# Sliding-window attention and a SiLU feed-forward: q and k of the first two batches loaded in two parts, with a new written order

## The chip, the cores and the metric

The kernel runs on one core of a Trainium2 chip. The metric is device time in microseconds (us) of one execution, the median over runs. Engines are called PE (TensorE, matmuls), PEld (its weight loads), ACT (ScalarE), DVE (VectorE), POOL (GpSimd) and SP (SyncE). POOL issues all loads and SP all stores.

## The reference

Causal attention in a window of 64 tokens, over 8 batches, 8 heads, 576 tokens and a head size of 64, is followed by a two-matrix feed-forward on the 4608 tokens:

```python
scores = scale * np.matmul(q, k.transpose(0, 1, 3, 2))
mask = (rel >= 0) & (rel < 64)              # rel = query position - key position
attn = softmax(np.where(mask, scores, -1e9))
x = np.matmul(attn, v)                      # -> [4608, 512], heads side by side
h = x @ w_in                                # w_in  [512, 2048]
return (h * sigmoid(h)) @ w_out             # w_out [2048, 512]
```

All inputs and the output are float32. The kernel loads its inputs with a cast to bfloat16.

## The kernel before

**Tiles.** A block is 64 tokens; a batch has 9 blocks, and all 8 batches make 72 blocks, numbered through. Blocks 0 to 8 are batch 0, and 9 to 17 batch 1. A token tile j is 512 tokens, or 8 blocks, so there are nine (tile 0 holds blocks 0 to 7, tile 1 blocks 8 to 15). Four heads form a quad; quad 0 and quad 1 are called a0 and a1 here.

**Attention.** A visit treats some blocks of one quad: `scores` (PE, L292; with an added mask from L285 in the first visits), four exponentials (`expo`, ACT, L307), `masking` (DVE, L314, where the mask was not added), `values` (PE, L323), `inverse` (DVE, L334), `normal` (DVE, L338) and `turn_out` (DVE, L442), which transposes the result into `xt`, the input of the feed-forward. Tiles 0 and 1 are visited in halves of four blocks, later tiles in eight. `values` needs v in a layout with two neighbouring blocks on the 128 partitions; for the first two batches `place_all` (L273, L275; on ACT or DVE) copies halves of the loaded v to make the other half of these pairs.

**Loads of q and k.** For batches 0 and 1, `load_quad` (L224) brings q or k of four heads in one load: partition p of a head's 32 gets 18 successive tokens. `turn_quad` then transposes it on DVE into `kT` (L255) or `qT` (L258). All blocks of that batch and quad depend on this one transpose. For later batches `load_head` (L227) brings one head at a time and `turn_blocks` (L265, L268) transposes four. `load_v`, `load_v_even` (L233 to L241) bring v, `load_w_in` (L245) and `load_w_out` (L248) the weights, each weight in eight loads of 256 KB as they lie in SBUF.

**Feed-forward.** Tile 0 takes the plain product: `first_plain` (PE, L450), 16 silus (ACT, L461), `second_plain` (PE, L464). The first four groups of `first_plain` are cut in two halves; the first half needs only quad 0 of the attention and the first half of w_in's rows. Tiles 1 to 8 take a scheme with seven products of half size in place of eight: `first_product` (PE, L507), `second_product` (PE, L519), with sums of the weights (`weight_sum1`, `weight_sum2`, DVE, L469, built once), of tokens (`token_sum1`, `token_sum2`, DVE, L485 to L496), copies and sums of partial results (`fork` L523, `join` L526) and silus (L529). The stores are at L533.

**The order.** Nothing is scheduled when the kernel runs. Each step is an operation with a number, an engine and dependencies, added to `Plan`; the string `ORDER` then names the operations in the order in which they are written to the engines' queues, with the PSUM banks (of eight) that each takes. `74P7` is operation 74, on PE, in bank 7. An engine works through its own operations in this order, and waits where a dependency isn't met. The string `LOADS` only numbers the loads and transposes of the start and adds them to the plan:

```python
LOADS = "p0-2 u0-4 i0-2 i2-4 i4-6 r0-1 i6-8 o0-2 v0-1 o2-3 r1-2 o3-4 v1-2 u4-5 o4-5 v2-4 o5-8 v4-5"
```

Here p is q and k of batch 0 (by quads), r those of batch 1, u and v the value blocks of batches 0 and 1, i w_in, and o w_out. Before the first scores PE is given filler matmuls (`warm`, L895), which compute nothing that is used. A check of the inverses at the end may call `general()`, a slow path for extreme inputs, which these inputs don't take.

Of the kernel before, what the change touches and what calls it, by code (L numbers as in the profile page):

```python
# [29 lines left out]
class Plan:  # L30
# [88 lines left out]
def kernel(ctx, tc, q, k, v, w_in, w_out, out):  # L119
# [414 lines left out]

    SOFT, ROWS, VACT, F1, F2 = 0.69, 1, 2, 1, 1
    turned, placed = {}, {}
    score_ops, value_ops, turn_ops = {}, {}, {}
    cast_ops = []  # L540
# [447 lines left out]
```

## Time and profile before

| what | value |
|---|---|
| median of 3 runs | 277.21 us (275.41 to 277.24) |
| profiled execution | 276.81 us, its span 275.0 us |
| PE busy | 264.7 us (96%) |
| DVE busy | 214.0 us (78%) |
| ACT busy | 195.6 us (71%) |
| POOL busy | 129.7 us (47%) |
| loads (POOL's queue) | 21.51 MB, in 96128 packets |

In rows of the timeline the first number is the start in us from the start of the span, the second the duration, then the engine, the line, the operation and what it writes and reads; "x24" counts merged instructions, and brackets hold the idle time of the engine before the row and what ended it. The granted PE clock is 1.000 throughout.

### The profile page before, as it was taken

To read this page: it belongs to the slowest core of one execution; us is meant where nothing else is said; L and a number is where in the kernel's file an instruction comes from. 1 tells how busy PE (TensorE), PEld (TensorE's weight loads), DVE (VectorE), ACT (ScalarE), POOL (GpSimd) and SP (SyncE) were. 2 spreads that over 40 slices of the span, in tenths; PEclk is the share of its full clock that TensorE was granted. 3 is DMA by queue.
4 is the path that set the end of the run, shared out by engine and by line. 5 is a ranking of instruction groups with operands and counts; after the bars stand their busy time and mean duration, and the time that the engine had idled before them with its cause. 6 is when DMAs were issued, how large, how long until landed. Compare 5 with 4: busy or idle time off the path is not lost.

```text
span 275.0 us, 10018 instructions
## 1 busy us (share of the span) xinstructions
PE 264.7 (96%) x4335; PEld 218.0 (79%) x4342; DVE 214.0 (78%) x426; ACT 195.6 (71%) x361; POOL 129.7 (47%) x194
## 2 busy tenths in 40 slices
PE   7978999999999999999999999999999999999993
PEld 2557844688888888888888888888888888888882
DVE  3757578999996898889799999988867967824741
ACT  1555993699749993987499958893888489537910
POOL 7944566988959758596387335940000000000000
PEclk9999999999999999999999999999999999999999
DMA  6999999999999959999979998990400040003004
GB/s 106 167 190 210 198 191 172 144 198 157 118 151 209 127 56 97 242 122 87 93 179 159 83 126 122 136 121 2 155 0 2 6 155 0 2 29 127 0 2 157
DMA packets 101631, 31.62 MB, mean 115 GB/s; under 512 B 92368, under 2 KB 95440, under 8 KB 101584
## 3 DMA queue, kind: packets, MB, share of 16 engines
q0 software_dynamic: 96128, 21.51, 86.1%
q1 hardware_dynamic: 5456, 9.44, 9.7%
q8 instruction: 35, 0.57, 0.9%
q14 instruction: 12, 0.10, 0.1%
HBM read 42.99 MB, written 9.44 MB: 191 GB/s over the span
## 4 chain that ended last, share of the span: by engine, by line
PE 88%; ACT 4%; DVE 4%; issue 1%; ACTq 0%
PE room L519 36%; PE room L507 35%; PE room L292 4%; PE room L323 4%; PE room L450 4%; PE room L895 4%; PE room L464 2%; ACT es L307 2%; DVE o L338 1%; ACT L307 1%; ACT g L461 1%; DVE es L314 1%; DVE xt L442 1%; PE room L285 1%; ACT L461 0%
## 5 line engine op out<-in xcount | busy, mean ns | idle before, releaser
L529 ACT ACTIVATE g<-room 128x512 bf16<-128x512 f32 x96 | 53.6, 605 | 4.5 <-PE room L507 4.1
L507 PEld LDWEIGHTS <-wsum 128*128 128x128 bf16 x512 | 49.9, 98 | 7.2 <-issue 1.0
L519 PEld LDWEIGHTS <-gsum 128*128 128x128 bf16 x512 | 49.1, 98 | 6.2 <-DVE gsum L496 0.2
L507 PE MATMUL room<-xsum,wsum 128*128 128x256 bf16 x384 | 53.3, 272 | 0.5 <-ACT es L307 0.3
L307 ACT ACTIVATE es<-room 128x512 bf16<-128x512 f32 (+1 forms) x88 | 39.1, 533 | 14.2 <-PE room L292 9.6
L519 PE MATMUL room<-wsum,gsum 128*128 128x256 bf16 x384 | 48.4, 273 | 0.0
L507 PEld LDWEIGHTS <-w_in_sb 128*128 128x128 bf16 x384 | 37.2, 98 | 4.7
L519 PEld LDWEIGHTS <-g 128*128 128x128 bf16 x384 | 36.7, 98 | 4.6
L526 DVE TENSOR_TENSOR room<-room,part 128x512 f32<-128x512 f32 (+1 forms) x41 | 27.8, 684 | 13.7 <-ACT part L523 3.5
L227 POOL DMA_DIRECT2D nat<-in_k_dram x48 | 30.0, 631 | 15.1 <-DVE kT L265 11.4
L507 PE MATMUL room<-xt,w_in_sb 128*128 128x256 bf16 x256 | 36.8, 273 | 0.0
L519 PE MATMUL room<-w_out_sb,g 128*128 128x256 bf16 x256 | 35.7, 273 | 0.0
L227 POOL DMA_DIRECT2D nat<-in_q_dram x48 | 29.9, 637 | 9.7 <-DVE qT L268 6.1
L523 ACT COPY ot<-room 128x512 f32<-128x512 f32 (+1 forms) x23 | 13.3, 582 | 28.6 <-PE room L519 21.5
L235 POOL DMA_DIRECT2D vv<-in_v_dram x32 | 29.6, 940 | 5.0 <-DMA nat<-in_k_dram 1.7
L523 ACT COPY room<-room 128x512 f32<-128x512 f32 x40 | 23.3, 592 | 12.1 <-PE room L507 10.8
L526 DVE TENSOR_TENSOR fin<-room,part 128x512 f32<-128x512 f32 x32 | 21.6, 683 | 9.0 <-PE room L507 6.1
L523 ACT COPY part<-room 128x512 f32<-128x512 f32 x40 | 23.6, 598 | 6.4 <-PE room L519 3.2
L241 POOL DMA_DIRECT2D vv<-in_v_dram x24 | 22.3, 934 | 12.0 <-PE room L323 11.5
L314 DVE TENSOR_TENSOR es<-es,strip 128x1024 bf16<-128x1024 bf16 (+1 forms) x36 | 21.9, 626 | 6.7 <-ACT es L307 6.4
L338 DVE TENSOR_TENSOR o<-room,recips 128x896 bf16<-128x896 f32 (+2 forms) x36 | 25.9, 726 | 0.8
L496 DVE TENSOR_TENSOR gsum<-g,gsum 128x512 bf16<-128x512 bf16 x64 | 25.1, 415 | 0.4
(75 smaller groups left out, 376.8 us busy)
## 6 DMA issues: line engine op xcount, KB each, us to landing
out_dram<-ot SPq DMA_DIRECT2D x16, 512.0 KB, 3.9
vv<-in_v_dram POOLq DMA_DIRECT2D x56, 128.0 KB, 5.0
nat<-in_k_dram POOLq DMA_DIRECT2D x48, 72.0 KB, 4.0
nat<-in_q_dram POOLq DMA_DIRECT2D x48, 72.0 KB, 3.7
w_in_sb<-in_moe_w_in_dram POOLq DMA_DIRECT2D x8, 256.0 KB, 9.2
w_out_sb<-in_moe_w_out_dram POOLq DMA_DIRECT2D x8, 256.0 KB, 9.0
nat<-in_k_dram POOLq DMA_DIRECT2D x4, 288.0 KB, 8.0
nat<-in_q_dram POOLq DMA_DIRECT2D x4, 288.0 KB, 8.2
```

The costliest lines, as they stand in the source:

```text
L227: queue[e].dma_start(out=nats[b % 2][a][kk][32 * h:32 * h + 32].rearrange("p (n x) -> p n x", n=NB), in_=(q, k)[kk][b, 4 * a + h].rearrang ...
L235: queue[e].dma_start(out=vv[b % 2][:, :, 2 * g + 1, 0:D], in_=v[b, :, 128 * g:128 * g + 128].rearrange("h p d -> p h d"))
L241: queue[e].dma_start(out=vv[b % 2][:, :, 2 * g, 0:D], in_=v[b, :, 128 * g - 64:128 * g + 64].rearrange("h p d -> p h d"))
L307: nc.scalar.activation(out=es_part(a, blocks)[:, h], in_=banks[bank.idx][:, 0:64 * n], func=ACTF.Exp, scale=scale)
L314: nc.vector.tensor_mul(t, t, strip[:, s:s + n].rearrange("k n i -> k (n i)").unsqueeze(1).to_broadcast([128, 2, 64 * n]))
L338: nc.vector.tensor_mul(out, at_values(bank, n)[:, :, :, 0:D], recips[:, w:w + 2 * n].rearrange("k (t n) -> k t n", t=bank.wide).unsqueeze( ...
L496: nc.vector.tensor_sub(out=dst[2 * i - 1], in0=g(1, 2 - i), in1=dst[i - 1])
L507: nc.tensor.matmul(banks[bank.idx][:, 256 * i:256 * i + 256], lhsT=lhs(z, i), rhs=rhs(z), start=(start and i == 0 and z == 0), stop=(z == ...
L519: nc.tensor.matmul(banks[bank.idx][:, 256 * m:256 * m + 256], lhsT=lhs(m, i), rhs=rhs(i), start=(start and i == 0 and m == 0), stop=(stop ...
L523: copies[e](out=dst, in_=src)
L526: nc.vector.tensor_add(out=dst, in0=bank, in1=part)
L529: nc.scalar.activation(out=g_tile(pair, 256 * t, 256 * t + 256), in_=src.rearrange("k (f t) -> k f t", f=2), func=ACTF.Silu)
```

## The change

**Two parts.** `load_quad` and `turn_quad` get a part. Of the 18 tokens per partition the first load would have held, the main part of batch 0 holds 16 (512 tokens, blocks 0 to 7), the rest 2 (64 tokens, block 8). For batch 1 the main part holds 14 (448 tokens, blocks 9 to 15) and the rest 4 (128 tokens, blocks 16 and 17). So eight loads and eight transposes are added (k and q, two quads, two batches), and each block depends on its own part alone. A rest of batch 0 writes 256 bytes per partition, one of batch 1 512.

**Weight sums in wider pieces.** `weight_sum1` and `weight_sum2` work on 1024 elements per partition in place of 512: 8 operations each in place of 16.

**A new order.** All of `ORDER` is different. The loads as POOL issues them at the start (q1 a0 is q of batch 1, quad 0; w_in 0-2/1 is columns 0 to 511 of the second half of the rows; v0 g2 is the third value load of batch 0; "rest" is a second part):

```
before: k0 a0, q0 a0, k0 a1, q0 a1, v0 g2, v0 g0, v0 g1, v0 g3, w_in 0-2/0, 0-2/1, 2-4/0, 2-4/1, 4-6/0, 4-6/1,
        k1 a0, q1 a0, w_in 6-8/0, 6-8/1, w_out 0, 2, k1 a1, w_out 4, v1 g0, q1 a1, v1 g1, w_out 6, v0 g4, w_out 8,
        v1 g2, w_out 10, v1 g3, w_out 14, 12, then batch 2
after:  k0 a0, q0 a0, k0 a1, q0 a1, v0 g2, v0 g0, v0 g1, v0 g3, w_in 0-2/0, 2-4/0, k0 a1 rest, w_in 0-2/1, 2-4/1,
        q1 a0 rest, w_in 4-6/1, q0 a1 rest, w_in 6-8/1, 4-6/0, q0 a0 rest, w_in 6-8/0, k1 a0, q1 a0, k0 a0 rest,
        w_out 0, 2, v0 g4, w_out 4, v1 g2, k1 a1, q1 a1, w_out 6, v1 g1, w_out 8, v1 g3, v1 g0, w_out 10,
        k1 a1 rest, w_out 14, 12, q1 a1 rest, k1 a0 rest, then batch 2
```

PE at the start (S scores, V values, a0 and a1 the quads, numbers the blocks; "first" is `first_plain`, "second" `second_plain`):

```
before: 24 fillers, S a0 0-3, S a0 4-7, 7 fillers, S a1 0-3, S a1 4-7, 4 fillers, V a0 0-3, V a1 0-3, V a0 4-7,
        first (2 halves, with 1 filler), V a1 4-7, first ..., S a0 8-11, first (4 groups), second of tile 0 with
        S a0 12-15, S a1 8-11, V a0 8-11, V a1 8-11, V a0 12-15, S a1 12-15, V a1 12-15 between them
after:  23 fillers, S a0 0-3, S a0 4-7, 4 fillers, S a1 0-3, S a1 4-7, 4 fillers, V a0 0-3, 2 fillers, V a1 0-3,
        V a0 4-7, V a1 4-7, 1 filler, first (4 halves), all other first, second of tile 0 with S a0 12-15,
        S a0 8-11, S a1 12-15, S a1 8-11, V a0 8-11, V a0 12-15, V a1 8-11, V a1 12-15 between them
```

On ACT the exponentials of batch 1 stood among the silus of tile 0 (12 silus, 3 exponentials, 4 silus, the other exponentials); now all 16 silus come first. On DVE the main transposes of batch 1 and the rests of batch 0 now stand among the sums of w_in and the masks of blocks 8 to 15; q of quad 0 is the first rest of batch 1 to be transposed there, and the other three (k of quad 1, k of quad 0, q of quad 1, in this order) stand among the normalizations of blocks 8 to 15. The later tiles keep their operations; their order and banks differ in many places.

The diff without `ORDER`, cut to its core:

```diff
-    wsum1 = [keep.tile([128, 4, 2, 256], BF16, name=f"wsum1{u}") for u in range(4)]
+    wsum1 = [keep.tile([128, 4, 2, 512], BF16, name=f"wsum1{w}") for w in range(2)]
...
-    def load_quad(e, b, a, kk):
-        queue[e].dma_start(out=nats[b % 2][a][kk], in_=(q, k)[kk][b, 4 * a:4 * a + 4].rearrange("h (p c) d -> (h p) (c d)", c=18))
+    def quad_part(b, rest):
+        most = (16, 14)[b]
+        return (most, 18 - most) if rest else (0, most)
+
+    def load_quad(e, b, a, kk, rest):
+        c0, c = quad_part(b, rest)
+        queue[e].dma_start(out=nats[b % 2][a][kk][:, 64 * c0:64 * c0 + 64 * c],
+                           in_=(q, k)[kk][b, 4 * a:4 * a + 4, 32 * c0:32 * c0 + 32 * c].rearrange("h (p c) d -> h p (c d)", c=c))
...
+    def turn_quad(b, a, kk, rest):
+        c0, c = quad_part(b, rest)
+        src = nats[b % 2][a][kk][:, 64 * c0:64 * c0 + 64 * c].bitcast(FP32)
         if kk:
+            n = 64 + 576 * (b % 2) + 32 * c0
+            dst = kT[a][:, n:n + 32 * c].rearrange("x t y -> x (t y)").bitcast(FP32)
+            nc.vector.transpose(out=dst.rearrange("x (p c) -> x c p", c=c), in_=src.rearrange("x (c w) -> x c w", c=c))
...
-    def weight_sum1(i, u):
-        sum_op(i, [wsum1[u][:, n] for n in range(4)], w_in_part(0, 0, u), w_in_part(0, 1, u), w_in_part(1, 0, u), w_in_part(1, 1, u))
+    def weight_sum1(i, w):
+        part = lambda h, c: w_in_sb[2 * h + w][:, 2 * c:2 * c + 2]
+        sum_op(i, [wsum1[w][:, n] for n in range(4)], part(0, 0), part(0, 1), part(1, 0), part(1, 1))
...
-        for x in range(NB):
+            c0, c = quad_part(b, rest)
+            op = p.add({"DVE": 0.07 + 0.063 * c}, lambda _: turn_quad(b, a, kk, rest), deps + old, prio, tag="turn")
+            part = range(c0 // 2, (c0 + c) // 2)
+        for x in part:
             turned.setdefault((b, a, x), []).append(op)
...
-    LOADS = "p0-2 u0-4 i0-2 i2-4 i4-6 r0-1 i6-8 o0-2 v0-1 o2-3 r1-2 o3-4 v1-2 u4-5 o4-5 v2-4 o5-8 v4-5"
+    LOADS = "p0-2 u0-1 o0-1 u1-4 i0-2 i2-4 i4-6 i6-8 o1-2 r0-1 v0-1 o2-3 x0-1 v1-2 r1-2 o3-4 v2-3 x1-2 o4-5 v3-4 u4-5 o5-7 y0-1 v4-5 o7-8 y1-2"
...
+        elif what[0] in "xy":
+            load_rows(int(what[0] == "y"), 10 + 20 * (what[0] == "y"), range(lo, hi), True)
```

In `LOADS` x is the rest of batch 0 and y that of batch 1.

More of the change, by code (lines that the diff above doesn't have):

```diff
@@ L248, in load_w_out @@
         queue[e].dma_start(out=w_out_sb[:, f0:f1], in_=w_out[128 * f0:128 * f1].rearrange("(p z) m -> p z m", z=f1 - f0))
-    def turn_quad(b, a, kk):
-        src = nats[b % 2][a][kk].bitcast(FP32)
+    def turn_quad(b, a, kk, rest):
+        c0, c = quad_part(b, rest)
+        src = nats[b % 2][a][kk][:, 64 * c0:64 * c0 + 64 * c].bitcast(FP32)
         if kk:
-            n = 576 * (b % 2)
-            dst = kT[a][:, 64 + n:640 + n].rearrange("x t y -> x (t y)").bitcast(FP32)
-            nc.vector.transpose(out=dst.rearrange("x (p c) -> x c p", c=18), in_=src.rearrange("x (c w) -> x c w", c=18))
-        else:
-            dst = qT[a][:, b % 2].rearrange("x t y z -> x t (y z)").bitcast(FP32)
-            nc.vector.transpose(out=dst.rearrange("x t (p c) -> x c t p", c=9), in_=src.rearrange("x (c t w) -> x c t w", c=9, t=2))
+            n = 64 + 576 * (b % 2) + 32 * c0
+            dst = kT[a][:, n:n + 32 * c].rearrange("x t y -> x (t y)").bitcast(FP32)
+            nc.vector.transpose(out=dst.rearrange("x (p c) -> x c p", c=c), in_=src.rearrange("x (c w) -> x c w", c=c))
+        else:
+            dst = qT[a][:, b % 2, :, 16 * c0:16 * c0 + 16 * c].rearrange("x t y z -> x t (y z)").bitcast(FP32)
+            nc.vector.transpose(out=dst.rearrange("x t (p c) -> x c t p", c=c // 2), in_=src.rearrange("x (c t w) -> x c t w", c=c // 2, t=2))
     def turn_blocks(b, a, kk):
@@ L499, in first_product @@
         a = lambda h, c: lambda z, i: w_in_part(h, c, u)[:, z, i:256:2]
-        s = lambda n: lambda z, i: wsum1[u][:, n, z, i:256:2]
+        s = lambda n: lambda z, i: wsum1[u // 2][:, n, z, 256 * (u % 2) + i:256 * (u % 2) + 256:2]
         b = lambda c, t: lambda z: xts[j % NXT][:, 2 * c + z, 256 * t:256 * t + 256]
@@ L533, in store @@
         queue[e].dma_start(out=out[r0 + 128 * m0:r0 + 128 * m1, lo:hi].rearrange("(m p) d -> p m d", p=128), in_=ot[:, m0:m1, lo:hi])
-    SOFT, ROWS, VACT, F1, F2 = 0.69, 1, 2, 1, 1
+    SOFT, F1, F2 = 0.69, 1, 1
     turned, placed = {}, {}
@@ L540, with turn_plan @@
     cast_ops = []
-    def turn_plan(b, a, kk, i, deps, prio):
+    def turn_plan(b, a, kk, rest, deps, prio):
         old = score_ops.get((b - 2, a), []) + ([c_k] if kk and b == 0 else [])
-        if i is None:
+        if rest is None:
             op = p.add({"DVE": 0.7}, lambda _: turn_blocks(b, a, kk), deps + old, prio, tag="turn")
+            part = range(NB)
         else:
-            op = p.add({"DVE": 1.2}, lambda _: turn_quad(b, a, kk), deps + old, prio, tag="turn")
-        for x in range(NB):
+            c0, c = quad_part(b, rest)
+            op = p.add({"DVE": 0.07 + 0.063 * c}, lambda _: turn_quad(b, a, kk, rest), deps + old, prio, tag="turn")
+            part = range(c0 // 2, (c0 + c) // 2)
+        for x in part:
             turned.setdefault((b, a, x), []).append(op)
@@ L568, with load_rows @@
     ADD1, PD = False, 2
-    LOADS = "p0-2 u0-4 i0-2 i2-4 i4-6 r0-1 i6-8 o0-2 v0-1 o2-3 r1-2 o3-4 v1-2 u4-5 o4-5 v2-4 o5-8 v4-5"
+    LOADS = "p0-2 u0-1 o0-1 u1-4 i0-2 i2-4 i4-6 i6-8 o1-2 r0-1 v0-1 o2-3 x0-1 v1-2 r1-2 o3-4 v2-3 x1-2 o4-5 v3-4 u4-5 o5-7 y0-1 v4-5 o7-8 y1-2"
     EARLY, EP, FULL, SPLIT, FILL = 0, 20, 4, 4, 512
-    def load_rows(b, prio, quads=(0, 1)):
+    def load_rows(b, prio, quads=(0, 1), rest=False):
         for a in quads:
             for kk in (1, 0):
-                ld = soft(SOFT, lambda e, a=a, kk=kk: load_quad(e, b, a, kk), turn_ops.get((b - 2, a, kk), []), dma=("s2304", 128))
-                turn_plan(b, a, kk, 0, [ld], prio + 0.1 * a)
+                ld = soft(SOFT, lambda e, a=a, kk=kk: load_quad(e, b, a, kk, rest), turn_ops.get((b - 2, a, kk), []),
+                          dma=("s%d" % (128 * quad_part(b, rest)[1]), 128))
+                turn_plan(b, a, kk, rest, [ld], prio + 0.1 * a)
     def load_heads(b, prio, quads=(0, 1)):
@@ L873, in load_w @@
             for a in range(NQ):
-                ld = soft(SOFT, lambda e, a=a: load_w_in(e, a, 256 * lo, 256 * hi), dma=("s2048", 256) if hi - lo == 4 else ("s1024", 128 * (hi - lo)))
+                ld = soft(SOFT, lambda e, a=a: load_w_in(e, a, 256 * lo, 256 * hi), dma=("s%d" % (512 * (hi - lo)), 256))
                 for pi in range(lo, hi):
@@ L906 @@
     exps += visit([12, 13, 14, 15], 47, added=ADD1)
-    for u in range(4):
+    for w in range(2):
         for i in range(4):
-            wsums2[u].append(p.add({"DVE": dve(512, 1920)}, lambda _, i=i, u=u: weight_sum2(i, 2 * u, 2 * u + 2), wout + cast_ops + wsums2[u][-1:], 110 + u, tag="wsum"))
+            op = p.add({"DVE": dve(1056, 1920)}, lambda _, i=i, w=w: weight_sum2(i, 4 * w, 4 * w + 4), wout + cast_ops + wsums2[2 * w][-1:], 110 + 2 * w, tag="wsum")
+            for u in (2 * w, 2 * w + 1):
+                wsums2[u].append(op)
     n_b = [2]
@@ L914, in load_until @@
             b, prio = n_b[0], 100 * j - 80
-            rows = load_rows if b <= ROWS else load_heads
-            rows(b, prio)
+            load_heads(b, prio)
             load_windows(b)
@@ L925 @@
         if j == 1:
-            for u in range(4):
+            for w in range(2):
                 for i in range(4):
-                    wsums1[u].append(p.add({"DVE": dve(512, 1920)}, lambda _, i=i, u=u: weight_sum1(i, u),
-                                           [x for lst in win.values() for x in lst] + cast_ops + wsums1[u][-1:], 140 + u, tag="wsum"))
+                    op = p.add({"DVE": dve(1056, 1920)}, lambda _, i=i, w=w: weight_sum1(i, w),
+                               [x for lst in win.values() for x in lst] + cast_ops + wsums1[2 * w][-1:], 140 + 2 * w, tag="wsum")
+                    for u in (2 * w, 2 * w + 1):
+                        wsums1[u].append(op)
         if j >= F1:
```

120 rows, old and new, of the table ORDER are left out of this document.

## The prediction

> **What bounds the kernel now.** I read the page first: busy time of the engines, then the slices.
>
> ```profile
> PE 264.7 (96%) x4335; PEld 218.0 (79%) x4342; DVE 214.0 (78%) x426; ACT 195.6 (71%) x361; POOL 129.7 (47%) x194
> PE   7978999999999999999999999999999999999993
> ```
>
> TensorE (PE) is the bound, but not evenly: the slices below 9 (6.9 us each) are the first, third and fourth and the last. The list of waits, from 56 us to the end and for PE alone, shows how little is left after the start:
>
> ```profile
> PE room L507 <- ACT es L307: 0.3, 1, 0.3
> PE room L323 <- DVE o L338: 0.2, 1, 0.2
> PE room L507 <- issue: 0.2, 1, 0.2
> ```
>
> That is 0.7 us in 219 us. The change takes no matmul out of that part, so it can only lose there. What can be won lies before the first product of token tile 1 (L507), whose position the timeline of PE gives. So I followed PE through the first 53 us:
>
> ```profile
> 1.39 7.60 PE L895 MATMUL room<-fill 128*128 128x512 bf16 x24 [1.39 <-DVE fill L213]
> 14.00 1.04 PE L895 MATMUL room<-fill 128*128 128x512 bf16 x4
> 14.96 0.67 PE L323 MATMUL room<-vv,es 128*32 128x65 bf16 x44
> 17.21 0.60 PE L323 MATMUL room<-vv,es 128*32 128x65 bf16 x52 [1.58 <-issue]
> 21.32 0.60 PE L450 MATMUL room<-xt,w_in_sb 128*128 128x256 bf16 x4 [0.43 <-DVE xt L442]
> 22.42 7.91 PE L450 MATMUL room<-xt,w_in_sb 128*128 128x256 bf16 x71 [0.51 <-DVE xt L442]
> 30.27 0.42 PE L292 MATMUL room<-qT,kT 32*128 32x64 bf16 x32
> 30.61 3.67 PE L450 MATMUL room<-xt,w_in_sb 128*128 128x256 bf16 x32
> 34.12 4.02 PE L464 MATMUL room<-w_out_sb,g 128*128 128x512 bf16 x16
> 48.09 2.33 PE L464 MATMUL room<-w_out_sb,g 128*128 128x512 bf16 x10
> 52.23 1.04 PE L507 MATMUL room<-xt,w_in_sb 128*128 128x256 bf16 x8
> ```
>
> The columns are start, duration, what ran, and in brackets the idle time before. L895 is filler. First products of tile 0 (L450) run gapless from 22.42 to 34.12, second products (L464) to 52.23. A 256-wide matmul there takes 3.51/32 = 0.110 us (30.61 to 34.12), a 512-wide one about 0.226 (ten in the 2.33 us from 48.09, less the 0.07 by which the modelled end of the last runs into the next form). ScalarE (ACT) and VectorE (DVE) in that stage:
>
> ```profile
> 30.98 1.28 ACT L307 ACT_TABLE_LOAD   x1
> 33.23 1.28 ACT L461 ACT_TABLE_LOAD   x1
> 34.52 2.06 ACT L461 ACTIVATE g<-room 128x512 bf16<-128x512 f32 x4
> 36.59 1.28 ACT L307 ACT_TABLE_LOAD   x1
> 48.28 1.21 ACT L307 ACTIVATE es<-room 128x256 bf16<-128x256 f32 x4 [4.32 <-DVE xt L442]
> 49.27 0.75 DVE L314 TENSOR_TENSOR es<-es,strip 128x512 bf16<-128x512 bf16 x2
> 50.90 0.21 DVE L334 RECIPROCAL recips<-room 128x8 f32<-128x8 f32 x1 [0.19 <-PE room L323]
> 51.14 0.73 DVE L338 TENSOR_TENSOR o<-room,recips 128x512 bf16<-128x512 f32 x1
> 51.91 0.45 DVE L442 STREAM_TRANSPOSE xt<-o 128x256 f32<-128x256 f32 x1
> 52.39 0.69 DVE L485 TENSOR_TENSOR xsum<-xt 128x1024 bf16<-128x1024 bf16 x1
> ```
>
> ACT changes its table three times because exponentials of batch 1 stand between silus of tile 0, and the last four exponentials come only at 48.28; mask, values, normalization and crossing then end at 52.36, when the first product of tile 1 may start.
>
> **The loads.** POOL issues them, and from 15 us on it waits for an older load to land before each issue; the steps give the queue's pace (the last row is the page's table of issues, with the median from issue to landing):
>
> ```profile
> 20.24 0.54 POOL L248 DMA_DIRECT2D w_out_sb<-in_moe_w_out_dram  x1 [0.77 <-DMA w_in_sb<-in_moe_w_in_dram]
> 21.51 0.53 POOL L224 DMA_DIRECT2D nat<-in_k_dram  x1 [0.73 <-DMA w_in_sb<-in_moe_w_in_dram]
> 24.18 0.89 POOL L235 DMA_DIRECT2D vv<-in_v_dram  x1 [0.88 <-DMA nat<-in_k_dram]
> 25.62 0.54 POOL L224 DMA_DIRECT2D nat<-in_q_dram  x1 [0.55 <-DMA nat<-in_q_dram]
> 35.60 0.54 POOL L248 DMA_DIRECT2D w_out_sb<-in_moe_w_out_dram  x1 [0.55 <-DMA nat<-in_q_dram]
> 36.43 0.53 POOL L248 DMA_DIRECT2D w_out_sb<-in_moe_w_out_dram  x1 [0.30 <-DMA vv<-in_v_dram]
> 49.39 1.79 POOL L227 DMA_DIRECT2D nat<-in_q_dram  x3
> ...
> w_out_sb<-in_moe_w_out_dram POOLq DMA_DIRECT2D x8, 256.0 KB, 9.0
> ```
>
> 256 KB take 1.27 us (20.24 to 21.51), 288 KB 1.44 (24.18 to 25.62). So the bytes are the price, and the change moves the same bytes: 32 KB taken from each load of batch 0 is 0.16 us, 64 KB of batch 1 is 0.32. A rest piece has no row. Below I take its bytes (0.16, 0.32), above 0.60, the step of 72 KB loads in pieces of 256 bytes (1.79/3, 49.39); I take 0.2 and 0.35, near the bytes, since those 72 KB hold more pieces than a rest. The Trainium skill, page "DMA: Bandwidth & Descriptors", section "Specifications", speaks against the split: transfers under 512 B fall below line rate by read-modify-write, and batch 0's rests are 256 B per partition. At twice the bytes' time this would cost 4 x 0.16 = 0.6 us of queue, by estimate; no run here shows a rest yet.
>
> **Part 1, to the end of tile 0's first products.** The DVE rows that bear on it:
>
> ```profile
> 5.58 1.25 DVE L255 STREAM_TRANSPOSE kT<-nat 128x576 f32<-128x576 f32 x1 [0.48 <-DMA nat<-in_k_dram]
> 9.89 1.23 DVE L258 STREAM_TRANSPOSE qT<-nat 128x576 f32<-128x576 f32 x1
> 54.46 0.78 DVE L265 STREAM_TRANSPOSE kT<-nat 128x576 f32<-128x576 f32 x1
> 44.87 0.29 DVE L275 COPY vv<-vv 64x512 bf16<-64x512 bf16 x1
> 49.94 0.75 DVE L469 TENSOR_TENSOR wsum<-w_out_sb 128x512 bf16<-128x512 bf16 x2
> ```
>
> The fourth load of batch 0 lands 4 x 0.16 = 0.64 us earlier and its transpose of 16/18 takes 1.1 instead of 1.23, so q of quad 1 is ready at 11.12 - 0.64 - 0.13 = 10.35. The new order has 23 fillers, two scores, 4 fillers, two scores, 4 fillers; before it was 24, 7, 4. At 0.25 each (1.04/4) the second pair of scores starts about 1.0 earlier (11.4), the first values at 14.0 instead of 14.96; their v blocks land 0.64 earlier and are placed by 13.4. The 1.58 us break inside the values (44 of 96 matmuls, then 52) has no wait of the program behind it; I leave it where it is in the instruction count. It would be worth 1.58 if it went. New: all four values come before any first product, ending at about 17.5, and 16 first half-products follow that need only the first half of w_in's rows. So PE has one wait left, about 0.3, for the crossing of blocks 4 to 7 (the break ends at about 16.8, and three more rounds of reciprocal, normalization and crossing on DVE, 50.90 to 52.36 = 1.46 each, end at 21.2). With one more filler the 128 matmuls end at 17.5 + 0.25 + 128 x 0.110 + 0.3 = 32.1. Before: 34.12, less 0.35 for the scores at 30.27, so 33.8. Gain 1.7. The w_out load put forward in the list is issued behind w_in in the written order, so it delays nothing here.
>
> **Part 2, to the first product of tile 1.** All 16 silus now run before any exponential of batch 1: two table loads fewer, 2 x 1.28 of ACT. The last silus follow PE's 32.1 and end at about 33.35, the table is in at 34.65, four exponentials (1.21) are done at 35.85. PE by then does second products: 18 of them and one scores (0.35) put the second scores at 32.1 + 18 x 0.226 + 0.35 = 36.5, and their exponentials end at 36.9 + 1.2 = 38.1. From there DVE has, in its order, without a gap: 7 masks (0.37 each, 0.75/2), 2 wide weight sums (0.69, as the 128x1024 row), 6 placements (0.29), 4 rest transposes, 4 reciprocals (0.24 with the gap to the next start), 4 normalizations (0.75), 4 crossings (0.47). The rest transposes have no row: the two transposes 128x256 in 0.45 and 128x576 in 0.78 give 1.03 ns an element and 0.19 fixed, so 0.25 for 64 elements and 0.32 for 128; below, 0.14 and 0.28 by 1.25/576; above 0.45 each, the smallest one in the trace. I take 0.25 + 3 x 0.32, by that line. Sum: 2.6 + 1.4 + 1.7 + 1.2 + 1.0 + 3.0 + 1.9 = 12.8, so the last crossing ends at 50.9. PE's own second products would be through at 50.4. The first product of tile 1 starts at 50.9 instead of 52.23: **gain 1.3**. The bounds of the rests (-0.3, +0.6 on DVE) leave 0.7 to 1.6.
>
> The wide weight sums: two narrow ones cost 0.75, one wide 0.69, so 16 pairs save about 1 us of DVE in all, half of it before 50.9 and counted. The Trainium skill, page "VectorE: DVE Perf Modes", section on the TRN2 errata, says every instruction from SBUF pays a fixed latency; the trace agrees, with 0.19 us in the transposes. By it the 8 added transposes lose what the sums win.
>
> **Part 3, the rest.** The same matmuls follow in another order, with PE the bound. Loads of batch 2 come behind eight small ones, but POOL had to wait there anyway (the bracketed waits), and my estimate from POOL's 0.6 us steps is that the last v block of tile 2's first visit, load 77 of the new order and 71 of the old, still lands 1 to 2 us before its values. I cost this part at 0; if that cover is gone, those values wait 1 to 2 us.
>
> **Sum.** The profiled execution took 276.81 us, its span is 275.0. 276.81 - 1.3 = 275.5. The median of the runs, 277.21, stands 0.4 above the profiled one, so I predict 275.8 on its scale.
>
> **Rivals.** (a) *More than that*: DVE's queue doesn't bind, and PE alone does: 32.1 + 64 x 0.226 + 4 x 0.35 + 4 x 0.43 = 49.7, a gain of 2.5; with half of the 1.58 break gone, 3.3: 273.9. For it: DVE had idle time before 45 us. Against: in the new order turns and placements of v, loaded later than before, stand ahead of the reciprocals. (b) *Nothing*: the later v block 0 of batch 1 (its load is moved from before to behind w_out's fifth) or a wait in the changed later order takes back the 1.3: 277.2. For it: PE after 56 us has nothing left to win and margins to lose. (c) *Slower*: the last rest, k of batch 1's quad 0, stands on DVE's queue ahead of the third reciprocal. With the same bytes ahead of it I have it landing at about 45.4 (36.43 + 9.0, the last w_out load) and DVE there at 46.8, 4.1 before the end of its chain. If a rest costs 0.95 instead of about 0.25 (a v load's 128 KB take 0.83, 35.60 to 36.43), the eight of them land it at 51.0, DVE stands 4.2 us, and the first product moves to 55.1, 2.9 later than before: 280.1. It decides from 0.6 us a rest, where 8 x 0.35 eats the 1.4 of margin and the 1.3 of gain. Against it: bytes set every step above.
>
> **How the numbers follow.** Forecast 0.41 (its own range 274.8 to 276.8), (a) 0.24, (b) 0.19, (c) 0.16. 1%, about what a measurement of this kernel tells from no change, is 2.8 us, or 274.4 and 280.0. Faster: (a) and a little of the forecast, 0.25. Slower: most of (c), and a little of (b) where a wait in the later order costs over 3 us, 0.16. Same: 0.59. The range 273.2 to 279.8 leaves out the ends of (a) and (c).
>
> **What would show it.** Right: the first L507 at about 50.9; two table loads fewer between 30 and 40 us; fillers 34; L450 gapless from about 21.3 to 32; rest transposes of 0.25 to 0.35; PE waits after 56 us still under 1 us. Wrong: a DVE wait for nat between 40 and 50 us (c); PE waits on L323 or L292 after 56 us (b); the 1.58 break gone or doubled; L464 held by w_out.

## The result and the profile after

The changed kernel takes 283.60 us (median of 4 runs, 282.92 to 283.97), the kernel before 276.75 us (4 runs, 275.41 to 277.24) on the same chip: a ratio of 1.0236, with a 95% interval from 1.0203 to 1.0268. It is slower by 6.9 us, where 275.8 us was forecast. The profiled execution took 283.97 us with a span of 282.3, 7.3 us more than before. In the new line numbers first products of tile 0 are L458 (before L450), second products L472 (L464), products of tile 1 and later L516 and L528 (L507, L519), scores L300 (L292), values L331 (L323), the transposes of k and q L263 and L266 (L255, L258).

The page of the changed kernel, engines and slices (7.1 us each):

```profile
PE 264.9 (94%) x4332; PEld 217.7 (77%) x4340; DVE 217.3 (77%) x427; ACT 188.2 (67%) x350; POOL 136.2 (48%) x202
PE   8296998899999999999999999999999999999992
PEclk9779999999999999999999999999999999999998
```

PE's busy time is as before (264.9 against 264.7), so the 7 us are time in which PE stands. The second slice shows where: 2 tenths. The third row is the granted clock, which was full throughout before; here it falls to 0.7 in that slice and the next. PE's timeline gives the positions:

```profile
13.51 0.62 PE L300 MATMUL room<-qT,kT 32*128 32x64 bf16 x32 [5.21 <-DVE qT L266]
23.96 2.89 PE L458 MATMUL room<-xt,w_in_sb 128*128 128x256 bf16 x25 [0.44 <-DVE o L346]
27.57 11.40 PE L458 MATMUL room<-xt,w_in_sb 128*128 128x256 bf16 x103 [0.72 <-DVE xt L450]
38.81 1.24 PE L472 MATMUL room<-w_out_sb,g 128*128 128x512 bf16 x4
47.04 1.02 PE L472 MATMUL room<-w_out_sb,g 128*128 128x512 bf16 x4 [0.62 <-DMA w_out_sb<-in_moe_w_out_dram]
51.60 0.43 PE L331 MATMUL room<-vv,es 128*32 128x65 bf16 x32 [0.58 <-DVE o L346]
58.09 1.04 PE L516 MATMUL room<-xt,w_in_sb 128*128 128x256 bf16 x8
...
276.06 0.60 PE L528 MATMUL room<-w_out_sb,gsum 128*128 128x256 bf16 x4
```

The last matmuls of the kernel before, in its timeline of PE:

```profile
269.76 0.60 PE L519 MATMUL room<-w_out_sb,gsum 128*128 128x256 bf16 x4
```

So the 7.3 us of span divide: the first product of tile 1 starts at 58.09 in place of 52.23 (+5.9); from there to PE's last matmul it takes 218.6 in place of 218.1 (+0.4); from PE's end to the end of the span 5.6 in place of 4.6 (+1.0). The first part is the case. PE waits 5.21 us for q of quad 0. On DVE, the four main transposes of batch 0:

```profile
10.82 1.03 DVE L263 STREAM_TRANSPOSE kT<-nat 128x512 f32<-128x512 f32 x1 [5.07 <-DMA nat<-in_k_dram]
12.37 1.09 DVE L266 STREAM_TRANSPOSE qT<-nat 128x512 f32<-128x512 f32 x1 [0.51 <-DMA nat<-in_q_dram]
13.96 0.97 DVE L263 STREAM_TRANSPOSE kT<-nat 128x512 f32<-128x512 f32 x1
14.80 1.06 DVE L266 STREAM_TRANSPOSE qT<-nat 128x512 f32<-128x512 f32 x1
```

Before, they started at 5.58, 7.06, 8.48 and 9.89. The first load of the program, with an empty queue ahead of it and 256 KB in place of 288, lands 5.2 us later. The view of the DMA issues, taken for the first 5 us, has the median from issue to landing in its last column; of the kernel before:

```profile
nat<-in_k_dram POOLq DMA_DIRECT2D x2, 288.0 KB, 5.0
nat<-in_q_dram POOLq DMA_DIRECT2D x2, 288.0 KB, 5.8
```

and of the changed kernel:

```profile
nat<-in_k_dram POOLq DMA_DIRECT2D x2, 256.0 KB, 9.8
nat<-in_q_dram POOLq DMA_DIRECT2D x2, 256.0 KB, 10.5
```

The same view for 2 to 12 us, before and then after, shows that it isn't a full queue that holds them:

```profile
DMA packets 3967, 1.61 MB, mean 161 GB/s; under 512 B 3455, under 2 KB 3455, under 8 KB 3967
```

```profile
DMA packets 2274, 0.97 MB, mean 97 GB/s; under 512 B 1829, under 2 KB 1829, under 8 KB 2274
```

The DMA engines move less, not more. The trace records sixteen completions for each load. Before, those of the first load of k come between 4.7 and 5.6 us, all together. After, twelve come between 3.5 and 3.7 and four between 10.2 and 10.8. I read this so: **twelve engines had nothing to carry, and four carried all 128 rows**. Of q's completions, issued next, eight come by 4.4 us, four between 10.4 and 11.0 and the last four between 12.0 and 12.3: its rows lie on four other engines, and four were still at those of k. The diff shows what could do that: the source was `(h p) (c d)`, one run of 128 equal steps; with 512 of 576 tokens the heads no longer join, and the source is `h p (c d)`, 4 steps on the outside.

### The profile page after: what moved, and what is told of

It reads as the page before. It is cut to its first block, busy times and chain, and to the rows that moved or that the text cites. A ratio compares the mean times of both kernels' runs of the same rounds, so it can differ in the third digit from the quotient of the medians.

```text
span 282.3 us, 10005 instructions
## 1 busy us (share of the span) xinstructions
PE 264.9 (94%) x4332; PEld 217.7 (77%) x4340; DVE 217.3 (77%) x427; ACT 188.2 (67%) x350; POOL 136.2 (48%) x202
## 4 chain that ended last, share of the span: by engine, by line
PE 71%; DMA 14%; ACT 5%; DVE 4%; POOL 3%; issue 2%; DVEq 0%; ACTq 0%; POOLq 0%
PE room L528 33%; PE room L516 31%; DMA nat<-in_q_dram 4%; DMA nat<-in_k_dram 3%; PE room L331 3%; DMA vv<-in_v_dram 3%; DMA w_in_sb<-in_moe_w_in_dram 3%; PE room L300 3%; ACT g L538 3%; PE room L472 1%; POOL nat L230 1%; DVE es L322 1%; ACT es L315 1%; ACT room L532 1%; POOL vv L242 1%
## 5 line engine op out<-in xcount | busy, mean ns | idle before, releaser
L516 PEld LDWEIGHTS <-wsum 128*128 128x128 bf16 x512 | 49.6, 98 | 6.9 <-issue 0.7
L516 PE MATMUL room<-xsum,wsum 128*128 128x256 bf16 x384 | 54.3, 273 | 0.2
L528 PEld LDWEIGHTS <-gsum 128*128 128x128 bf16 x512 | 48.7, 98 | 7.2 <-DVE gsum L502 0.4
L315 ACT ACTIVATE es<-room 128x512 bf16<-128x512 f32 (+1 forms) x88 | 39.7, 529 | 17.6 <-PE room L300 17.1
L528 PE MATMUL room<-wsum,gsum 128*128 128x256 bf16 x384 | 49.3, 273 | 0.0
L516 PEld LDWEIGHTS <-w_in_sb 128*128 128x128 bf16 x384 | 37.4, 98 | 4.6
L528 PEld LDWEIGHTS <-g 128*128 128x128 bf16 x384 | 36.9, 98 | 4.5
L516 PE MATMUL room<-xt,w_in_sb 128*128 128x256 bf16 x256 | 37.4, 273 | 0.0
L528 PE MATMUL room<-w_out_sb,g 128*128 128x256 bf16 x256 | 35.8, 273 | 0.0
L234 POOL DMA_DIRECT2D nat<-in_k_dram x48 | 29.3, 616 | 8.8 <-DVE kT L273 6.0
L242 POOL DMA_DIRECT2D vv<-in_v_dram x32 | 28.8, 905 | 9.3 <-PE room L331 6.8
L532 ACT COPY ot<-room 128x512 f32<-128x512 f32 (+1 forms) x17 | 9.7, 577 | 33.7 <-PE room L528 21.3
L532 ACT COPY room<-room 128x512 f32<-128x512 f32 x40 | 23.9, 597 | 12.0 <-PE room L516 5.5
L248 POOL DMA_DIRECT2D vv<-in_v_dram x24 | 21.5, 914 | 8.6 <-PE room L331 8.6
```

The costliest lines, as they stand in the source:

```text
L234: queue[e].dma_start(out=nats[b % 2][a][kk][32 * h:32 * h + 32].rearrange("p (n x) -> p n x", n=NB), in_=(q, k)[kk][b, 4 * a + h].rearrang ...
L242: queue[e].dma_start(out=vv[b % 2][:, :, 2 * g + 1, 0:D], in_=v[b, :, 128 * g:128 * g + 128].rearrange("h p d -> p h d"))
L248: queue[e].dma_start(out=vv[b % 2][:, :, 2 * g, 0:D], in_=v[b, :, 128 * g - 64:128 * g + 64].rearrange("h p d -> p h d"))
L315: nc.scalar.activation(out=es_part(a, blocks)[:, h], in_=banks[bank.idx][:, 0:64 * n], func=ACTF.Exp, scale=scale)
L516: nc.tensor.matmul(banks[bank.idx][:, 256 * i:256 * i + 256], lhsT=lhs(z, i), rhs=rhs(z), start=(start and i == 0 and z == 0), stop=(z == ...
L528: nc.tensor.matmul(banks[bank.idx][:, 256 * m:256 * m + 256], lhsT=lhs(m, i), rhs=rhs(i), start=(start and i == 0 and m == 0), stop=(stop ...
```

## Experiments

Theory A: a load runs on as many DMA engines as its source has outer steps, and that, in the four first loads, is the loss. Rivals: R, that eight more loads and transposes cost, as in the prediction's rival (c); O, that the new order does.

**The part loads spread again.** Same bytes, partitions, order and transposes; the source steps evenly:

```diff
-  in_=(q, k)[kk][b, 4 * a:4 * a + 4, 32 * c0:32 * c0 + 32 * c].rearrange("h (p c) d -> h p (c d)", c=c))
+  in_=(q, k)[kk][b, 4 * a:4 * a + 4].rearrange("h (p c) d -> (h p) (c d)", c=18)[:, 64 * c0:64 * c0 + 64 * c])
```

> The changed kernel with one edit: a part load takes its 16 and 2 (or 14 and 4) tokens out of each partition's 18 successive tokens, so that its source has 128 equal steps in place of 4 heads of 32 partitions. Bytes, partitions, order and transposes stay; which token stands in which column of batches 0 and 1 is changed, and so is that part of the computation. Theory A (a part load runs on 4 of the 16 DMA engines, 32 rows one after the other on each): the main loads of batch 0 land as before (5.6 to 9.9 us), the first product of tile 1 starts at 50 to 53 us, the kernel takes 275 to 278 us. Rival R (the eight added loads and their transposes are what costs, however they are laid out): still 282 to 284 us. Rival O (the new order of tile 1 and later costs): the start comes back, but 279 to 282 us.

Measured: 277.99 us, ratio to before 1.0031 (0.9994 to 1.0068). Its timelines of DVE and of PE:

```profile
5.55 1.04 DVE L263 STREAM_TRANSPOSE kT<-nat 128x512 f32<-128x512 f32 x1 [0.46 <-DMA nat<-in_k_dram]
...
9.37 1.12 DVE L266 STREAM_TRANSPOSE qT<-nat 128x512 f32<-128x512 f32 x1
```

```profile
1.39 7.85 PE L910 MATMUL room<-fill 128*128 128x512 bf16 x23 [1.39 <-DVE fill L213]
9.61 0.42 PE L300 MATMUL room<-qT,kT 32*128 32x64 bf16 x32
18.96 2.89 PE L458 MATMUL room<-xt,w_in_sb 128*128 128x256 bf16 x25
22.57 11.40 PE L458 MATMUL room<-xt,w_in_sb 128*128 128x256 bf16 x103 [0.72 <-DVE xt L450]
33.81 1.24 PE L472 MATMUL room<-w_out_sb,g 128*128 128x512 bf16 x5
52.09 1.04 PE L516 MATMUL room<-xt,w_in_sb 128*128 128x256 bf16 x8
```

The loads are back at their old times, the 5.9 us are gone, and with them nearly all of the loss. R falls: all eight rests are still there. In this run a rest of batch 0 landed 0.17 to 0.23 us after the load ahead of it, one of batch 1 0.30 to 0.40.

**Whole loads in the new order.**

```diff
-        most = (16, 14)[b]
-        return (most, 18 - most) if rest else (0, most)
+        return (18, 0) if rest else (0, 18)      # and load_quad, turn_quad return at once for a rest
```

> The changed kernel with whole loads and whole transposes of q and k for batches 0 and 1, as before the change; the rests are not issued. The new order and the wide weight sums stay. Theory A: loads land as before, 275 to 278 us; against the spread part loads it tells what eight added small loads are worth: within 1 us if a rest costs its bytes, 3 us and more less if each costs 0.6 us of the queue. Rival O: 279 us or more. Blocks 8 of batch 0 and 16, 17 of batch 1 come earlier than they need here, the others later by 2/18 and 4/18 of a load.

Measured: 277.43 us, ratio 1.0005 (0.9971 to 1.0038). The first product of tile 1 starts at

```profile
51.64 1.04 PE L518 MATMUL room<-xt,w_in_sb 128*128 128x256 bf16 x8
```

O falls as the main cause. The new order with whole loads does neither good nor harm that this measurement tells from nothing, and the eight rests with their transposes make a difference of 0.6 us (277.99 against 277.43), where rival (c)'s price would have asked for 3 or more.

**The other way round: only the source's outer steps, put into the kernel before.**

```diff
-  in_=(q, k)[kk][b, 4 * a:4 * a + 4].rearrange("h (p c) d -> (h p) (c d)", c=18))
+  in_=(q, k)[kk][b, a:8:2].rearrange("h (p c) d -> h p (c d)", c=18))
```

> The kernel before with one edit: load_quad takes every second head, so that its four heads don't lie one behind the other in memory; bytes, number of loads, order and transposes stay. Quads hold other heads of q and k than of v, which changes what is computed. Theory A: the source now has 4 steps on the outside, the first load of k lands at 11 to 12 us in place of 5.6, the first product of tile 1 moves from 52 to 57 to 60 us, and the kernel takes 282 to 286 us without any other part of the change. Rivals R and O: 276.5 to 277.5 us, no difference.

Measured: 282.73 us, ratio 1.0217 (1.0144 to 1.0289), from DVE's first transpose on:

```profile
11.72 1.26 DVE L255 STREAM_TRANSPOSE kT<-nat 128x576 f32<-128x576 f32 x1 [6.02 <-DMA nat<-in_k_dram]
```

```profile
14.25 0.61 PE L292 MATMUL room<-qT,kT 32*128 32x64 bf16 x32 [5.24 <-DVE qT L258]
...
58.20 1.04 PE L507 MATMUL room<-xt,w_in_sb 128*128 128x256 bf16 x8
```

One line of one address, with no load added and the old order, makes the whole delay of the start: the same 5.2 us of PE, the same 58 us. (About 1 us of the changed kernel's loss isn't in it: 282.73 against 283.60.) So from both sides it is the shape of the source that makes the delay. Whether it is the number of its outer steps, and not only that it isn't one run, the next two runs ask.

**Its law: eight steps and two.** Both in the kernel before.

```diff
+  ap=[[288 * 64, 8], [17 * 64, 16], [1, 1152]]            # e6: 8 outer steps of 16 rows
+  ap=[[4 * 576 * 64, 2], [18 * 64, 64], [1, 1152]]        # e7: 2 outer steps of 64 rows
```

> The kernel before with one edit: the 128 rows of a whole load of q or k are told as 8 outer steps of 16 rows; two neighbouring rows overlap by one token and so some tokens differ, which changes what is computed. Theory A with its law (a load runs on as many engines as its source has outer steps, and a row of 2304 bytes takes an engine 0.26 us: 5.60 - 3.48 = 2.1 us for the 8 rows per engine of the kernel before, 11.71 - 3.48 = 8.2 us for the 32 rows with four steps): 16 rows each, the first load of k lands at 3.5 + 4.1 = 7.6 us, the fourth load at about 12.4 in place of 9.9, the kernel takes 279 to 280.5 us. Rival (any source that isn't one run is slow, whatever its steps): 11 to 12 us for the first load, and 282 to 283 us.

> The kernel before with one edit: each whole load of q or k takes two pairs of heads that lie apart, so that its 128 rows are two outer steps of 64; quads hold other heads of q and k than of v, which changes what is computed. Theory A with its law: 64 rows on each of two engines, the first load of k lands at 3.5 + 64 x 0.26 = 20 us, and the kernel takes 288 to 292 us. Rival (any source that isn't one run): 11 to 12 us for the first load, 282 to 283 us.

Measured: 277.88 us with eight (ratio 1.0034, 1.0014 to 1.0054) and 295.91 with two (1.0642, 1.0579 to 1.0705). The first transposes, with eight and with two:

```profile
7.05 1.26 DVE L256 STREAM_TRANSPOSE kT<-nat 128x576 f32<-128x576 f32 x1 [1.69 <-DMA nat<-in_k_dram]
```

```profile
16.86 1.26 DVE L256 STREAM_TRANSPOSE kT<-nat 128x576 f32<-128x576 f32 x1 [10.72 <-DMA nat<-in_k_dram]
```

With 16, 8, 4 and 2 engines the first load lands at 5.6, 7.1, 11.7 and 16.9 us. The rival, that any source which isn't one run is slow, asked for 11 to 12 in both and falls. The law holds in its order; its price per row doesn't stay at 0.26 us, since with eight engines it is (7.05 - 3.48)/16 = 0.22 and with two (16.86 - 3.48)/64 = 0.21. Both totals were missed. With eight steps I expected 279 to 280.5; the first product of tile 1 moved only from 52.23 to 53.45. With two I expected at most 292: I had reckoned with batch 0's loads alone, but batch 1's hold PE as well, in one place for 1.74 us and in another for 3.73:

```profile
57.71 0.51 PE L293 MATMUL room<-qT,kT 32*128 32x64 bf16 x24 [3.73 <-DVE qT L259]
```

The Trainium skill states this rule, page "DMA: Bandwidth & Descriptors", section "Why a DMA increments its semaphore by 16 and not by 1": the number of engines is the largest up to 16 that divides the slowest dimension of source and destination alike, and fewer than 16 are taken in turn from one transfer to the next. The traces agree in all four cases, as far as the completions tell, the turn included (with eight steps eight of k's completions come by 3.4 us and eight from 6.7 to 7.0, and with two steps fourteen by 4.2 and two at 16.4 and 16.8).

**Which batch.** Whole loads for batch 0, four-step part loads for batch 1:

```diff
-        most = (16, 14)[b]
+        most = (18, 14)[b]      # and for batch 0 the whole load's source; a rest of 0 tokens returns
```

> The changed kernel with whole loads and whole transposes for batch 0 alone; the loads of batch 1 stay in two parts with four outer steps. Theory A: PE has nothing to cover the first loads of batch 0, but work until 38 us before it scores blocks 8 to 15; so nearly all of the loss is batch 0's. The first product of tile 1 at 51.6 to 53 us, 277 to 279 us. Rival: the part loads of batch 1 hold up the queue behind them (w_out, v of batch 1) as much as those of batch 0 did, and 280 us or more are left.

Measured: 278.40 us, ratio 1.0050 (1.0018 to 1.0081). Two waits are left on PE that whole loads don't have:

```profile
39.69 0.42 PE L307 MATMUL room<-qT,kT 32*128 32x64 bf16 x32 [0.49 <-DVE qT L273]
47.77 0.59 PE L479 MATMUL room<-w_out_sb,g 128*128 128x512 bf16 x2 [0.69 <-DMA w_out_sb<-in_moe_w_out_dram]
52.58 1.04 PE L523 MATMUL room<-xt,w_in_sb 128*128 128x256 bf16 x8
```

Batch 1 is worth about 0.9 of the 5.9 us (52.58 against 51.64), a w_out load behind its loads included; batch 0 the other five, since PE has nothing but fillers to cover its loads. Its rival, 280 us or more, falls.

**The clock.** 20 fillers more, so that PE doesn't stand:

> The changed kernel with 20 more filler matmuls after its 23, so that PE is busy to about 13 us and doesn't stand 5.2 us. Theory A with a clock part: the granted clock stays at 1.0 from 10 to 20 us, where it was 0.60 and 0.72; the scores and fillers from 13.5 to 20.5 take their usual time (0.42 and 0.25 in place of 0.62 and 0.43), and the kernel gains 1 to 2 us: 281.6 to 282.6. Rival: the late loads alone set the start, through DVE's transposes and ACT's exponentials, and the clock is worth under 0.5 us: 283 to 284.

Measured: 284.03 us, ratio 1.0240 (1.0160 to 1.0319): no gain, as the rival had it. The windows (after the engines' busy times the granted clock, the DMA share, GB/s), of the changed kernel and with the fillers:

```profile
10.00:15.00 5.00, 1.49 (x36) 0.98 (x36) 3.46 (x7) 0.66 (x2) 2.15 (x3) 0.60 1.98 166
15.00:20.00 5.00, 4.66 (x110) 2.61 (x111) 2.12 (x5) 3.96 (x13) 4.24 (x6) 0.72 1.60 181
```

```profile
10.00:15.00 5.00, 4.89 (x88) 2.69 (x87) 3.57 (x7) 0.84 (x3) 2.28 (x4) 1.00 1.98 164
15.00:20.00 5.00, 4.20 (x108) 2.06 (x106) 2.05 (x5) 4.92 (x16) 3.47 (x5) 1.00 1.57 183
20.00:25.00 5.00, 3.53 (x109) 2.28 (x109) 3.87 (x10) 1.56 (x3) 3.44 (x5) 0.76 1.25 169
25.00:30.00 5.00, 4.28 (x35) 3.48 (x34) 2.33 (x5) 0.63 (x2) 3.88 (x7) 0.90 1.19 170
```

The clock does stay full where it had dropped, but it drops at 20 to 30 us instead, where the first products run, and by half as much: 5 x (0.24 + 0.10) = 1.7 us of clock are lost in place of 5 x (0.40 + 0.28) = 3.4. Even so the first product of tile 1 starts at 58.25, so the late loads set the start. How much the low clock adds of itself isn't settled.

**Why the cure brings no gain.** With spread loads q of quad 0 is turned at 7.89 us (6.79 + 1.10), but PE is in its fillers until 9.24. Five leading fillers taken out of that kernel, and out of the kernel before:

> The changed kernel with spread part loads (each partition's part out of its 18 successive tokens, so which token stands in which column of batches 0 and 1 is changed, and so is that part of the computation) and 5 of the 23 leading fillers taken out. With spread loads q of quad 0 was turned at 7.89 us, but PE was in its fillers until 9.24, so the first scores waited for the fillers and all behind them for the scores. Theory F (with spread loads the fillers eat the gain): first scores at about 8.4 in place of 9.6, the second pair 1.2 us earlier, first products of tile 0 from about 17.8 in place of 18.96, the first product of tile 1 at about 51 as forecast, 276.5 to 277.2 us where the same kernel with all fillers takes 278.0. Rival: the copies of v and ACT's exponentials set the values anyway; then the start moves by under 0.4 us.

> The kernel before with 5 of its 24 leading fillers taken out, nothing else. q of quad 0 is turned at 8.27, the fillers end at 8.99 and the first scores start at 9.36. Theory F: scores at about 8.6, and the chain behind them gains up to 0.7 us as far as it follows the exponentials: 276.3 to 277.0. Rival: no difference, since 11 more fillers stand behind the scores and hold PE until 14.96 anyway.

Measured: 277.77 us for the first (ratio to before 1.0034, 1.0002 to 1.0066) and 275.64 for the second (0.9970, 0.9938 to 1.0003). In the first the start does come, at the forecast place:

```profile
8.71 0.42 PE L300 MATMUL room<-qT,kT 32*128 32x64 bf16 x32
51.20 1.04 PE L516 MATMUL room<-xt,w_in_sb 128*128 128x256 bf16 x8
```

but it is lost behind it, as the table in the next section shows; the total, 277.77, lies above the 276.5 to 277.2 that I expected. And whether the fillers hold the scores differs from run to run. In every trace the first fillers take 0.43 us each and the later ones 0.22 (the page's row of the clock doesn't show it), and the switch comes anywhere from 4.1 to 7.3 us. So the same 23 fillers took 7.85 us with spread loads, but in the changed kernel and with whole loads

```profile
1.39 6.47 PE L910 MATMUL room<-fill 128*128 128x512 bf16 x23 [1.39 <-DVE fill L213]
```

```profile
1.39 6.96 PE L912 MATMUL room<-fill 128*128 128x512 bf16 x23 [1.39 <-DVE fill L213]
```

and with whole loads they end at 8.35, ahead of the scores, which wait for q. In the kernel before, scores at 8.88 in place of 9.36 run into a longer break among the values:

```profile
17.77 0.85 PE L323 MATMUL room<-vv,es 128*32 128x65 bf16 x47 [2.57 <-issue]
53.98 1.04 PE L507 MATMUL room<-xt,w_in_sb 128*128 128x256 bf16 x8
```

The break was 1.58 us and ended at 17.21. In both kernels a 16 KB packet of instructions comes through the DMA engines shortly ahead of its end (14.86 to 15.82 us before, 15.51 to 16.48 here; the break ends 1.4 and 1.3 us later). In eleven of the fourteen traces of this case, in the old order and the new, with up to 13 fillers out or 20 in, there is such a break, of 0.15 to 2.6 us: always behind the 221st to 223rd matmul of PE, and ending 1.2 to 1.5 us after that packet. In the other three PE comes to this place only later. So the break belongs to a place in the program, and I take it for PE waiting for its instructions there; an earlier start only meets it earlier. The profiled execution here took 278.79 us, 3.2 more than the median, and its granted clock fell behind the longer break (0.74 from 15 to 20 us, 0.92 to 25, both 1.00 before), so the 53.98 can't stand for the other executions. The 275.64 lies below the 276.3 to 277.0 that I expected, but whether it is a gain stays open: the interval holds 1.

**Two variants of the start of the kernel before.** Three copies of v moved from ACT to DVE and four fillers taken out; and that with nine fillers more out:

```diff
- 25A ... 26A ... 99P5 ... 100P0 ... 98P2 ... 102P1 ... 27A
+ 25D 26D ... 27D
```

> The kernel before with three copies of v (blocks of batch 0, 0.62 us each on ACT) moved to DVE (0.29 each), which had nothing to do from 11.1 to 15.5 us but four of them, and four fillers ahead of the first values taken out. ACT's exponentials of the first visits then end about 1.2 us earlier (14.4 in place of 15.6). If they and the fillers set the first values, these start at 14.0 in place of 15.0 and the kernel gains 0.5 to 1.2 us: 276.1 to 276.8. If the first products wait for DVE's crossings anyway, nothing: 277.3.

> The kernel before with three copies of v moved from ACT to DVE, 5 leading fillers, 4 of the 7 between the scores and 4 ahead of the first values taken out. Both holds of the start are gone at once: scores at about 8.6, the second pair when q of quad 1 is turned (about 11.3), values at about 13.6 in place of 14.96, first products 1 to 1.5 us earlier: 275.3 to 276.3. Rival: DVE, which takes all copies and then the normalizations, becomes the hold, and the time stays within 0.5 us of 277.

Measured: 276.63 us (ratio 0.9954, 0.9912 to 0.9997) and 276.69 (0.9997, 0.9966 to 1.0027). The first lies in its range and at the edge of what can be told; the second, which goes further in the same direction, does not gain, so no version here is shown to beat the kernel before by more than half a per cent. The mechanism isn't shown: in the profiled execution of the first (278.07 us, 1.4 above its median) ACT's first exponentials end at 16.07 where 14.4 was expected, and the first product of tile 1 starts at 53.50.

**Both orders joined.** Last, the changed order with whole loads and 18 leading fillers was taken up to the first product of tile 1, and the order of the kernel before from there. On record was 275.2 to 275.8 us if the two parts simply add, and 276.5 to 277.5 if the join costs a wait. Measured: 277.35 us against 276.39 before, ratio 1.0024 (1.0001 to 1.0048). This version returns wrong values, and why isn't known, so its time is only a hint. Its profile has the start (51.09) and the end (4.6 us behind PE) that were expected, but 219.6 us between them, with waits of 0.5 and 0.3 us of products of tile 1 for DVE.

## Why the prediction was wrong

**The step that failed** is the price of the loads: "the bytes are the price, and the change moves the same bytes". The steps of POOL from which I took it are steps between loads whose sixteen completions come close together. The main part, which I made cheaper by 0.16 us, is what became dear: the first one lands 5.2 us later, with its rows on four engines. With spread loads the term is right: the fourth transpose starts at 9.37 in place of 9.89, 0.5 us earlier where I had 0.64. I asked what a rest costs, since it was new, and not whether the main load was still the same load, though the diff shows its source lose the joined `(h p)`. The deciding question of rival (c), 0.6 us a rest, was put to the wrong load; spread rests cost close to their bytes (0.17 to 0.23 and 0.30 to 0.40 us, where I took 0.2 and 0.35), not twice as much. The rule of the Trainium skill told above would have given the four engines; I had weighed another sentence of that page.

**What held.** Two table loads fewer on ACT: between 10 and 50 us there are four in the old trace and two in the new. Rest transposes 0.21 to 0.40 us (forecast 0.25 to 0.35, so a little wider), wide sums 0.65 to 0.69 (0.69). PE's listed waits after the first product of tile 1 stay under 1 us. Three listed signs of wrong came: L472 is held by w_out (0.62); DVE waits 2.27 us, to 41.67, for k of batch 1, though for a main part and not for a rest; and the 1.58 us break is gone in the changed kernel, where PE comes to that place after the fetch.

**Part 1 was wrong also without the loads.** With spread loads q of quad 1 is turned at 10.49 (forecast 10.35), but the first products end at 33.8 where I had 32.1, though the break that I had left in at 1.58 us cost 0.16 there. I took the fillers for filling and not for work that can hold the scores: first scores 9.61, and the second pair at 13.07 in place of 11.4, because its banks wait for ACT's exponentials of the first pair. With five fillers fewer, 51.20 us came out against the forecast 50.9; that is near by chance, since there too the first products ended late and the second products took less than I had.

**Part 2 came out at the right length for another reason.** 12.8 us of DVE did not set the end. I had misread what the first product waits for: it reads only the first 256 tokens of tile 1, and before the change it already started at 52.23, ahead of the end of the last crossing at 52.36. With spread loads PE's second products run from 33.81 to 52.09, 18.3 us, with one wait of 0.57 us; forecast were 18.8. That is rival (a)'s rule, PE alone.

**Part 3 was not nothing.** From the profiles (us):

| kernel | first product of tile 1 | to PE's end | PE's end to span's end |
|---|---|---|---|
| before | 52.23 | 218.1 | 4.6 |
| old order, heads apart | 58.20 | 218.3 | 4.4 |
| old order, eight steps | 53.45 | 218.2 | 4.4 |
| old order, fewer fillers | 53.98 | 218.4 | 4.6 |
| changed | 58.09 | 218.6 | 5.6 |
| new order, spread loads | 52.09 | 218.8 | 5.6 |
| new order, whole loads | 51.64 | 219.5 | 5.2 |
| new order, spread, fewer fillers | 51.20 | 219.2 | 6.0 |
| both orders joined (wrong values) | 51.09 | 219.6 | 4.6 |

The rows are one execution each. In them the new order costs 0.4 to 1.4 us on PE, and 0.5 to 1.3 in the tail. For the tail there is a row: SP's last five stores, before and after.

```profile
267.78 4.11 SPq L533 DMA_DIRECT2D out_dram<-ot  x5
```

```profile
275.35 3.73 SPq L542 DMA_DIRECT2D out_dram<-ot  x5
```

They start 2.6 us ahead of PE's end before, and 1.3 ahead after (276.66 - 275.35), so more of the last writing lies behind PE; it is 2.6 in every trace with the old order at the end and 1.3 in every one with the new. The size isn't settled, since the old order with 13 fewer fillers has a tail of 6.0 in its profile too. That is close to rival (b), with part of its price in a place it did not name.

## What to carry to other kernels

When a load is cut, look at the shape of what is left of its source, not only at its bytes: count the equal steps on the outside and see whether two axes that used to join still do. If a transfer gets slower while the DMA engines are less busy than before, ask whether it is spread badly; here its completions, some at once and some late, showed it. And before costing a gain at the start, ask what else stands there by number: fillers, banks that are given back late, and the fetch of the program.

## What the hardware showed that I had not expected

- A load issued by POOL signals from all 16 engines, also from those that carry nothing: the first load with four outer steps had twelve signals at 3.5 us and four from 11.0 to 11.7. By an estimate from these times one row of 2304 bytes takes an engine (5.60 - 3.48)/8 = 0.26 us with 16 engines at work, 0.22 with eight and 0.21 with two.
- After a stand of 5.2 us PE's granted clock was 0.60 and then 0.72 for 10 us. Keeping PE busy with fillers moved that stretch by 10 us and halved its loss (0.76, then 0.90), but didn't take it away.
- Packets of 16 KB of instructions go through the DMA engines beside the loads. I take them for PE's program, since the break in PE's work stood behind the same matmul, the 221st to 223rd, in eleven traces, and ended 1.2 to 1.5 us after the first of these packets.
- The first fillers ran at half the rate of the later ones, and the switch came at 4.1 to 7.3 us, at another time in each trace. So the same fillers last up to 1.4 us longer from one execution to the next, which is as much as most of what was tried at the start.
